# Gated attention decode on one core: single K and V tiles take one half of the rows of their pair of tiles

## The chip, the cores and the metric

The kernel runs on one core of a Trainium2 chip. The metric is the device time of one execution in microseconds (us). Each comparison below runs the kernel and the kernel before on the same chip, in turn.

## The reference, cut to what matters

One token (`x`, 1 x 1024) goes through two branches. Branch A is grouped-query attention over a cache of 65,536 positions: 32 query heads, 4 groups of K and V, 128 values per head. Branch B is a small gated MLP. A sigmoid gate mixes them.

```python
q = (x @ wq).reshape(B, Sq, Hq, Dh).transpose(0, 2, 1, 3)
scores = einsum('bhqd,bhkd->bhqk', q, repeat(k_cache, 8)) * Dh ** -0.5
p = softmax(scores)                       # over the 65,536 positions k
o = einsum('bhqk,bhkd->bhqd', p, repeat(v_cache, 8))
a = o.transpose(0, 2, 1, 3).reshape(B, Sq, Hq * Dh) @ wo
return g * a + (1 - g) * b                # b: the MLP, g: the gate
```

What matters: the sum over `k` pairs the probability of position k with the V row of position k. Any order of the positions gives the same sum, so a kernel may spread them over the partitions as it likes, but it must spread K and V in the same way.

K and V of one group are 16.8 MB each, 134 MB in all. With the weights the kernel has to read 162 MB.

## The kernel before: what the change and the argument touch

PE is the engine for matrix products (PEld is its loading of weights), DVE the vector engine, ACT the scalar engine, POOL the GpSimd engine, and SP the engine that issues the loads; 16 DMA engines carry them out. SBUF is the core's own memory, 128 partitions wide. It holds one large buffer `kv` with 5 slots of 32 KiB per partition. A tile of K or V is 128 partitions x 128 positions x 128 values, one slot, 4 MB. A group has 4 tiles (j = 0 to 3) of K and 4 of V.

```python
def load_kv(src, g, j, at, n=1):
    k0, m = j * CT * P, n * CT                      # CT = P = 128
    v = load(src[0, g, k0:k0 + m * P, :].rearrange("(p c) d -> p (c d)", c=m),
             (m * DH,), at)
    return [v[:, i * CT * DH:(i + 1) * CT * DH] for i in range(n)]
...
for j in range(NT):                                 # group 0: four single loads of K
    k_tile(0, j, load_kv(A_k_cache, 0, j, (2, 1, 0, 3)[j])[0])
    ...
for g in range(1, G):
    for h in range(2):
        kn = load_kv(A_k_cache, g, 2 * h, 1 - h, 2)      # a pair of K tiles
        ...
        vn = load_kv(A_v_cache, g - 1, 2 * h, 3, 2)      # a pair of V tiles
        ...
for j, n, at in ((0, 2, 1), (2, 1, 3), (3, 1, 4)):  # V of group 3: one pair, two singles
    for i, vt in enumerate(load_kv(A_v_cache, G - 1, j, at, n)):
        v_tile(G - 1, j + i, vt)
```

A single load (n = 1) gives each partition 128 consecutive positions. A pair load (n = 2) gives each partition 256 consecutive positions, of which tile j takes the first 128 and tile j + 1 the other 128. So K of group 0 (singles) and V of group 0 (pairs) do not hold the same positions in the same place, and neither do tiles 2 and 3 of group 3 (K in a pair, V in singles).

`k_tile` transposes the tile in place in 32 x 32 blocks on DVE (four per tile) and multiplies it with the queries on PE into `s_ps`; ACT casts the scores to `sc`. `stats` finds the maximum, takes the exponentials and transposes the probabilities into `pt`. `v_tile` multiplies `pt` with the V tile. A slot comes free when the work on its tile is done, and only then is the next load for it issued, on one queue (SP), in program order.

## Time and profile before

| | before |
|---|---|
| time, median of the runs made with the prediction's result | 383.25 us (383.21 to 383.29, 4 runs) |
| bytes moved, mean rate over the span | 162.17 MB, 425 GB/s |
| load queue, share of 16 DMA engines' time | 98.8% |
| PE, DVE busy | 59%, 57% |

These are lines of the page of the kernel before. The two rows of figures cut the span into 40 slices: the mean busy share of the DMA engines in tenths (9 is 90% or more), and GB/s. "q1" is the load queue: its packets (a packet is one piece of a load that one DMA engine moves; a K or V load has one for each partition), MB, and the share of the 16 DMA engines' time. The next two lines are the chain of waits by engine and by line. The last two are groups of instructions: count, busy us and mean ns of one, then the idle time before them and what ended it.

```profile
span 381.3 us, 2581 instructions
...
PE 226.1 (59%) x1372; PEld 56.1 (15%) x796; DVE 218.5 (57%) x211; ACT 39.6 (10%) x55; POOL 4.4 (1%) x10
...
DMA  9999999999999999999999999999999999999995
GB/s 376 435 419 430 428 437 440 440 444 422 414 433 440 440 428 433 440 440 440 440 428 440 440 440 426 413 422 426 440 440 414 433 433 434 440 407 440 437 401 237
...
q1 hardware_dynamic: 4324, 162.01, 98.8%
...
DMA 60%; DVE 18%; PE 17%; issue 2%; ACT 1%; SPq 1%; DVEq 0%; ACTq 0%
DMA kv<-in_A_k_cache_dram 37%; PE s_ps L390 12%; DVE kv L383 12%; DMA kv<-in_A_wo_dram 9%; DMA kv<-in_A_wq_dram 7%; DMA kv<-in_A_v_cache_dram 7%; PE o_ps L436 3%; DVE pt L426 2%; DVE mx L385 1%; DVE o_sb L450 1%; PE q_ps L276 1%; ACT sc L42
...
L390 PE MATMUL s_ps<-kv,wt 128*128 128x512 bf16 x512 | 137.0, 424 | 87.6 <-DVE kv L383 87.4
L383 DVE STREAM_TRANSPOSE kv<-kv 128x2048 int32<-128x2048 int32 x64 | 142.7, 2280 | 58.7 <-DMA kv<-in_A_k_cache_dram 58.7
```

The loads bound this kernel, by this reading: the DMA row stands at 9 until the last slice, and no other engine comes near. The chain of waits still gives a third of its length to PE and DVE. Those pieces are what a load's slot waits for, while another load is already on the queue, so they show what has to happen in time, not what would shorten the run.

The table by stretches of the kernel before (us busy and instruction counts of each engine, the clock that PE was granted as a share of full speed, DMA share, GB/s) has the single loads of K of group 0 in the first stretch, the pair loads in the second and the single loads of V of group 3 in the third:

```profile
core 0: us, PE busy (x) PEld busy (x) DVE busy (x) ACT busy (x) POOL busy (x), PEclk, DMA share, GB/s
39.00:80.00 41.00, 24.84 (x120) 5.12 (x60) 33.23 (x30) 2.02 (x2) 0.00 (x0) 0.88 1.00 429
80.00:338.00 258.00, 163.75 (x889) 37.16 (x482) 166.28 (x123) 34.00 (x47) 0.00 (x0) 0.84 1.00 433
338.00:359.00 21.00, 12.57 (x98) 3.55 (x51) 1.77 (x6) 0.00 (x0) 0.00 (x0) 0.83 0.99 424
```

The DMA share is 0.99 to 1.00 in all three, and singles run at the rate of pairs within about 2%.

### The profile page before, as it was taken

The numbers are of one execution on the slowest core, as the hardware profiler recorded it, in microseconds if no ns is written. First come the engines' busy times: TensorE is split into PE (matmuls) and PEld (weight loads), VectorE is DVE, ScalarE is ACT, GpSimd is POOL, SyncE is SP. The second block draws the span as 40 slices with busy tenths as digits, with TensorE's granted clock in tenths as the row PEclk, the third lists the DMA queues.
The fourth block names the chain that finished last, engine by engine and source line by source line (L and its number), as shares of the span: only waits on it lengthen the run. The fifth ranks groups of instructions, "written<-read, shape, count | busy, mean of one in ns | idle before, by whom it ended". The sixth has DMA issues, their size and how long they took to land.

```text
span 381.3 us, 2581 instructions
## 1 busy us (share of the span) xinstructions
PE 226.1 (59%) x1372; PEld 56.1 (15%) x796; DVE 218.5 (57%) x211; ACT 39.6 (10%) x55; POOL 4.4 (1%) x10
## 2 busy tenths in 40 slices
PE   0433357677047934885388538762966197848354
PEld 0110011112011200111011101110211011212122
DVE  4241479996678406866986059669770497460040
ACT  1010001111601100114011001140100010500000
POOL 4000000000000000000000000000000000000000
PEclk9999859999759885999598959996899688969686
DMA  9999999999999999999999999999999999999995
GB/s 376 435 419 430 428 437 440 440 444 422 414 433 440 440 428 433 440 440 440 440 428 440 440 440 426 413 422 426 440 440 414 433 433 434 440 407 440 437 401 237
DMA packets 4375, 162.17 MB, mean 425 GB/s; under 512 B 520, under 2 KB 524, under 8 KB 908
## 3 DMA queue, kind: packets, MB, share of 16 engines
q1 hardware_dynamic: 4324, 162.01, 98.8%
q8 instruction: 8, 0.13, 0.1%
q14 instruction: 3, 0.02, 0.0%
q10 hardware_dynamic: 40, 0.01, 0.0%
HBM read 162.01 MB, written 0.00 MB: 425 GB/s over the span
## 4 chain that ended last, share of the span: by engine, by line
DMA 60%; DVE 18%; PE 17%; issue 2%; ACT 1%; SPq 1%; DVEq 0%; ACTq 0%
DMA kv<-in_A_k_cache_dram 37%; PE s_ps L390 12%; DVE kv L383 12%; DMA kv<-in_A_wo_dram 9%; DMA kv<-in_A_wq_dram 7%; DMA kv<-in_A_v_cache_dram 7%; PE o_ps L436 3%; DVE pt L426 2%; DVE mx L385 1%; DVE o_sb L450 1%; PE q_ps L276 1%; ACT sc L423 1%; DVE rowt L446 1%; ACT sc L401 1%; SPq L167 1%
## 5 line engine op out<-in xcount | busy, mean ns | idle before, releaser
L390 PE MATMUL s_ps<-kv,wt 128*128 128x512 bf16 x512 | 137.0, 424 | 87.6 <-DVE kv L383 87.4
L383 DVE STREAM_TRANSPOSE kv<-kv 128x2048 int32<-128x2048 int32 x64 | 142.7, 2280 | 58.7 <-DMA kv<-in_A_k_cache_dram 58.7
L436 PE MATMUL o_ps<-kv,pt 128*64 128x512 bf16 x512 | 60.4, 394 | 7.8 <-DMA kv<-in_A_v_cache_dram 7.8
L390 PEld LDWEIGHTS <-wt 128*128 128x128 bf16 x256 | 26.9, 105 | 199.1 <-issue 137.2
L401 ACT CAST sc<-s_ps 128x1024 bf16<-128x1024 f32 x16 | 16.2, 1012 | 253.7 <-PE s_ps L390 253.7
L436 PEld LDWEIGHTS <-pt 128*64 128x64 bf16 x256 | 15.8, 114 | 49.8 <-issue 47.7
L426 DVE STREAM_TRANSPOSE pt<-sc 128x1024 bf16<-128x1024 bf16 x16 | 18.6, 1217 | 6.8 <-ACT sc L423 6.8
L385 DVE TENSOR_REDUCE mx<-sc 128x1 f32<-128x1024 bf16 x12 | 14.5, 1210 | 8.9 <-ACT sc L401 8.9
L423 ACT ACTIVATE sc<-sc,nb 128x1024 bf16<-128x1024 bf16 x16 | 18.2, 1137 | 12.2 <-DVE nb L419 12.2
L446 DVE TENSOR_TENSOR rowt<-o_ps,own 128x1024 f32<-128x1024 f32 x4 | 4.8, 1195 | 23.8 <-PE o_ps L436 23.8
L456 PE MATMUL om_ps<-o_sb,hsel 128*32 128x128 f32 x8 | 2.3, 387 | 19.7 <-DVE o_sb L450 19.7
L405 DVE TENSOR_REDUCE mx<-sc 128x1 f32<-128x1024 bf16 x4 | 4.9, 1221 | 12.9 <-ACT sc L401 12.9
L276 PE MATMUL q_ps<-kv,xT 128*32 128x512 bf16 x64 | 6.8, 600 | 7.3 <-DMA kv<-in_A_wq_dram 7.3
L477 PE MATMUL out_ps<-kv,oa 128*32 128x256 bf16 x128 | 7.1, 377 | 4.1 <-DMA kv<-in_A_wo_dram 2.6
L276 PE MATMUL z_ps<-kv,xT 128*32 128x448 bf16 x64 | 6.4, 577 | 3.6 <-DMA kv<-in_B_w_in_dram 3.6
L343 DVE TENSOR_TENSOR rowt<-q_ps,own_b 128x512 f32<-128x512 f32 x2 | 1.3, 686 | 12.0 <-PE q_ps L276 12.0
L450 DVE TENSOR_REDUCE o_sb<-rowt 128x128 f32<-128x1024 f32 x4 | 7.5, 1872 | 0.1
L291 DVE TENSOR_TENSOR rowt<-z_ps,own_b 128x448 f32<-128x448 f32 x2 | 1.2, 620 | 8.4 <-PE z_ps L276 8.4
L276 PEld LDWEIGHTS <-xT 128*32 128x32 bf16 x64 | 3.0, 139 | 19.1 <-issue 19.0
L232 PE MATMUL xb_ps<-xg,spread 8*128 8x256 bf16 x1 | 0.4, 367 | 9.0 <-DMA xg<-in_gate_w_dram 9.0
L477 PEld LDWEIGHTS <-oa 128*32 128x32 bf16 x128 | 4.6, 127 | 6.5 <-issue 4.0
L520 ACT CAST out_sb<-out_ps 128x256 bf16<-128x256 f32 x1 | 0.4, 372 | 44.9 <-PE out_ps L477 44.9
(88 smaller groups left out, 54.9 us busy)
## 6 DMA issues: line engine op xcount, KB each, us to landing
kv<-in_A_k_cache_dram SPq DMA_DIRECT2D x4, 4096.0 KB, 26.7
kv<-in_A_wq_dram SPq DMA_DIRECT2D x2, 4096.0 KB, 32.7
kv<-in_A_v_cache_dram SPq DMA_DIRECT2D x2, 4096.0 KB
kv<-in_B_w_in_dram SPq DMA_DIRECT2D x2, 3584.0 KB, 14.9
kv<-in_A_wo_dram SPq DMA_DIRECT2D x1, 4096.0 KB
kv<-in_B_w_out_dram SPq DMA_DIRECT2D x1, 3584.0 KB
kv<-in_A_wo_dram SPq DMA_DIRECT2D x1, 2048.0 KB, 29.2
kv<-in_A_wo_dram SPq DMA_DIRECT2D x1, 1024.0 KB, 31.3
```

What stands on the lines that cost most here:

```text
L276: ins = nc.tensor.matmul(ps[t * B:(t + 1) * B, k * HN:k * HN + n], lhsT=xT[:, i * KH + c:i * KH + c + 1].to_broadcast([P, B]), rhs=w[:, c, ...
L383: nc.vector.transpose(out=kb[:, v * n:(v + 1) * n], in_=kb[:, v * n:(v + 1) * n])
L385: nc.vector.reduce_max(**late.pop())
L390: ins = nc.tensor.matmul(s_ps[:, k * HN:(k + 1) * HN], lhsT=wt[g % 2][:, v, b].rearrange("p a v h -> p (a v h)"), rhs=kx[:, b // 2, b % 2, ...
L401: nc.scalar.copy(out=sct[g, j][:], in_=s_ps[:])
L405: nc.vector.reduce_max(**late.pop())
L423: nc.scalar.activation(out=sct[g, j][:], in_=sct[g, j][:], func=ACT.Exp, scale=SCALE, bias=nb[:, 0:1], accum_out=lss[g][:, j:j + 1])
L426: nc.vector.transpose(out=ptt[g, j][:].rearrange("p c x -> p (c x)"), in_=sct[g, j][:])
L436: ins = nc.tensor.matmul(o_ps[g][hs, e, :], lhsT=ptt[g, j][:, 2 * u:2 * u + 2, :].rearrange("p c x -> p (c x)"), rhs=vx[:, 2 * u + e], sta ...
L446: nc.vector.tensor_tensor(out=om8, in0=o_ps[g][:].rearrange("p e (v d) -> p (e v) d", d=DH), in1=own_8[:].unsqueeze(2).to_broadcast([P, 2 ...
L450: nc.vector.tensor_reduce(out=o_sb[:], in_=om8.rearrange("p x d -> p d x"), axis=AX.X, op=ALU.add)
L477: nc.tensor.matmul(out_ps[t * B:(t + 1) * B, :], lhsT=vec[:, c0 + c:c0 + c + 1].to_broadcast([P, B]), rhs=w[:, c, t * NO:(t + 1) * NO], st ...
```

## The change

The intent is that every tile takes its half of the rows of its pair, whether it is loaded alone or with its partner, so that a partition holds the same positions for K and for V.

```diff
     def load_kv(src, g, j, at, n=1):
-        k0, m = j * CT * P, n * CT
-        v = load(src[0, g, k0:k0 + m * P, :].rearrange("(p c) d -> p (c d)", c=m),
-                 (m * DH,), at)
+        h, i = divmod(j, 2)
+        rows = src[0, g, 2 * h * CT * P:2 * (h + 1) * CT * P, :].rearrange(
+            "(p c) d -> p (c d)", c=2 * CT)
+        v = load(rows[:, i * CT * DH:(i + n) * CT * DH], (n * CT * DH,), at)
         return [v[:, i * CT * DH:(i + 1) * CT * DH] for i in range(n)]
```

Pair loads are as they were. The six single loads still bring 32 KiB to each partition, but from places 64 KiB apart (the pitch) instead of 32 KiB.

## The prediction

> **What bounds the kernel now.** The loads. The page's DMA row stands at 9 tenths or more in all 40 slices but the last, the load queue's packets fill 98.8% of the span of the 16 DMA engines, and 162.17 MB move in 381.3 us, 425 GB/s. The table by stretches gives a DMA share of 0.97 to 1.04 from 33 us to 346 us. PE is busy 59%, DVE 57%. The chain of waits is 60% DMA; its PE and DVE pieces (L390, L383) run while the queue holds the next load and matter only for how early a buffer comes free.
>
> **What the change does.** It touches no instruction on PE, DVE, ACT or POOL, no buffer and no wait, only source addresses of loads.
> - The 13 pair loads (6 of K, 7 of V) keep their source exactly: 64 KiB per partition, all contiguous.
> - The 6 single loads (4 of K for group 0, 2 of V for group 3) read 32 KiB per partition, as before, but from rows 64 KiB apart instead of 32 KiB: the same 4 MB, the same 128 packets of 32 KiB each.
>
> Its worth is correctness: before, K of group 0 and V of group 3's last two tiles came with 128 consecutive positions per partition while their partners came as halves of 256, so probabilities met the wrong V rows there. With nearly flat softmax weights the comparison with the reference probably hardly sees it.
>
> **What it costs.** Only a slower read from rows of wider pitch could cost time. The trace already has that pattern: the loads of A_wq and the 4 MB load of A_wo take 32 KiB of every 64 KiB. By the packet records, their packets take a median of 1213 ns (A_wq) and 1216 ns (A_wo); those of the contiguous single K and V loads 1216 ns; those of the pair loads 2421 ns for twice the bytes. All are 27 GB/s per engine. The Trainium skill ("DMA: Bandwidth & Descriptors", section "Latency and other measured facts") reports that large power-of-two row pitches slow HBM copies: 207 GB/s at 512 KiB, 164 at 2 MiB, 214 when padded. 64 KiB is below what it lists, and this trace shows no loss there. If the 6 loads' packets took 1% longer, 6 x 8 x 1.216 us = 58 us of DMA time would give 0.6 us (an estimate from those durations). It would be paid in full, as the queue is always full. I expect none.
>
> **Predicted: 383.25 us, 8 in 10 between 382.6 and 383.9.** Faster by over 2%: 0.01; within 2%: 0.98; slower by over 2%: 0.01.
>
> **What would show the steps right or wrong.**
> - Instruction count (2581) and packet counts (4324 on the load queue; 1152 of 32 KiB, 1664 of 64 KiB) unchanged.
> - Packets of 32 KiB keep a median within 1% of 1216 ns; from 33 to 72 us the queue still moves about 430 GB/s.
> - The chain keeps its shape: DMA about 60%, K loads about 37%.
> - Busy times of L390, L383, L436 unchanged within clock noise.
>
> **What would make it wrong.** If engines in lockstep at 64 KiB pitch collide in the HBM, the 6 loads' packets get longer (stretches 39 to 80 us and 338 to 359 us), by a few us in all at most. If the new source were cut into other descriptors, the packet counts would show it. If a K load landed so late that PE or DVE ran out of slack, later buffers would come free later, the queue's waits would grow and the DMA row would dip.

## The result

| | before | after |
|---|---|---|
| median | 383.25 us (4 runs) | 383.18 us (383.05 to 383.26, 4 runs) |
| ratio | | 0.9998, 95% interval 0.9981 to 1.0015 |

A ratio here is the mean time of one kernel's fast runs over that of the other's of the same rounds, so it is not quite the ratio of the medians.

The same lines of the page of the kernel after (its line numbers are one higher):

```profile
span 381.4 us, 2581 instructions
...
PE 232.4 (61%) x1372; PEld 56.8 (15%) x796; DVE 218.4 (57%) x211; ACT 39.6 (10%) x55; POOL 4.4 (1%) x10
...
DMA  9999999999999999999999999999999999999995
GB/s 376 439 426 416 433 436 440 436 461 429 400 426 440 440 435 426 440 440 440 440 428 440 440 440 433 428 427 406 433 440 428 426 433 427 440 411 436 440 405 230
...
q1 hardware_dynamic: 4324, 162.01, 98.7%
...
DMA 59%; PE 20%; DVE 16%; issue 2%; ACT 1%; SPq 1%; DVEq 0%; ACTq 0%
DMA kv<-in_A_k_cache_dram 37%; PE s_ps L391 15%; DVE kv L384 9%; DMA kv<-in_A_wo_dram 8%; DMA kv<-in_A_wq_dram 7%; DMA kv<-in_A_v_cache_dram 7%; PE o_ps L437 3%; DVE pt L427 2%; DVE mx L386 1%; DVE o_sb L451 1%; PE q_ps L277 1%; ACT sc L424
...
L391 PE MATMUL s_ps<-kv,wt 128*128 128x512 bf16 x512 | 142.1, 437 | 81.8 <-DVE kv L384 81.7
L384 DVE STREAM_TRANSPOSE kv<-kv 128x2048 int32<-128x2048 int32 x64 | 142.7, 2280 | 55.5 <-DMA kv<-in_A_k_cache_dram 55.5
```

And the same stretches:

```profile
core 0: us, PE busy (x) PEld busy (x) DVE busy (x) ACT busy (x) POOL busy (x), PEclk, DMA share, GB/s
39.00:80.00 41.00, 26.40 (x120) 5.29 (x60) 33.11 (x30) 2.03 (x2) 0.00 (x0) 0.83 1.00 429
80.00:338.00 258.00, 167.68 (x889) 37.69 (x482) 166.61 (x123) 34.01 (x47) 0.00 (x0) 0.83 1.00 433
338.00:359.00 21.00, 13.14 (x98) 3.62 (x51) 1.47 (x6) 0.00 (x0) 0.00 (x0) 0.83 0.99 424
```

The DMA shares and the GB/s of the three stretches are those of before to the last digit shown. Instructions and packets are as many as before. What moved is PE, and with it the parts of PE and DVE in the chain of waits: the score matmuls took 437 ns instead of 424 ns, 5.1 us more in all, in a run whose mean granted clock was 0.82 instead of 0.855. The same file in e11, at a mean clock of 0.863, took 427 ns, so most of this is a difference between runs and not the change. The span did not follow it (381.4 us in both runs of the changed kernel, 381.3 us before).

The trace also records each packet of the load queue. Sorted by size and order of start they fall into the loads, and this table gives the median time of one packet:

| packets | before | after |
|---|---|---|
| 32 KiB, A_wq (pitch 64 KiB in both) | 1213 ns | 1213 ns |
| 32 KiB, K of group 0 (pitch 32 KiB, then 64 KiB) | 1216 ns | 1216 ns |
| 32 KiB, V of group 3 (pitch 32 KiB, then 64 KiB) | 1216 ns | 1216 ns |
| 64 KiB, pairs of K and V | 2421 ns | 2421 ns |

The times of the runs alone leave room for about 0.6 us of loss, which is what 1% longer packets in these six loads would cost. The packets exclude it: they have the same median in both, to the nanosecond.

### The profile page after: what moved, and what is told of

It reads as the page before. It is cut to its first block, busy times and chain, and to the rows that moved or that the text cites. A ratio compares the mean times of both kernels' runs of the same rounds, so it can differ in the third digit from the quotient of the medians.

```text
span 381.4 us, 2581 instructions
## 1 busy us (share of the span) xinstructions
PE 232.4 (61%) x1372; PEld 56.8 (15%) x796; DVE 218.4 (57%) x211; ACT 39.6 (10%) x55; POOL 4.4 (1%) x10
## 3 DMA queue, kind: packets, MB, share of 16 engines
q1 hardware_dynamic: 4324, 162.01, 98.7%
## 4 chain that ended last, share of the span: by engine, by line
DMA 59%; PE 20%; DVE 16%; issue 2%; ACT 1%; SPq 1%; DVEq 0%; ACTq 0%
DMA kv<-in_A_k_cache_dram 37%; PE s_ps L391 15%; DVE kv L384 9%; DMA kv<-in_A_wo_dram 8%; DMA kv<-in_A_wq_dram 7%; DMA kv<-in_A_v_cache_dram 7%; PE o_ps L437 3%; DVE pt L427 2%; DVE mx L386 1%; DVE o_sb L451 1%; PE q_ps L277 1%; ACT sc L424 1%; DVE rowt L447 1%; ACT sc L402 1%; SPq L167 1%
## 5 line engine op out<-in xcount | busy, mean ns | idle before, releaser
L391 PE MATMUL s_ps<-kv,wt 128*128 128x512 bf16 x512 | 142.1, 437 | 81.8 <-DVE kv L384 81.7
L437 PE MATMUL o_ps<-kv,pt 128*64 128x512 bf16 x512 | 61.6, 399 | 7.7 <-DMA kv<-in_A_v_cache_dram 7.7
```

What stands on the lines that cost most here:

```text
L391: ins = nc.tensor.matmul(s_ps[:, k * HN:(k + 1) * HN], lhsT=wt[g % 2][:, v, b].rearrange("p a v h -> p (a v h)"), rhs=kx[:, b // 2, b % 2, ...
L437: ins = nc.tensor.matmul(o_ps[g][hs, e, :], lhsT=ptt[g, j][:, 2 * u:2 * u + 2, :].rearrange("p c x -> p (c x)"), rhs=vx[:, 2 * u + e], sta ...
```

## The experiments

Theory 1 says: the queue is always full, a packet's time depends on its bytes and not on the distance between rows, so nothing changes. Rival 2 says: a wider pitch does cost, but six loads and a doubling are too little to be seen. Rival 3 says: the engines set the time and these six loads have slack, so even a slower load would not have been seen. All edits are against the kernel after, if not said otherwise. Four kernels besides the detectors compute something wrong (e2, e3, e4 and e7).

### e1: pitch 128 KiB for all K and V loads

```diff
-        h, i = divmod(j, 2)
-        rows = src[0, g, 2 * h * CT * P:2 * (h + 1) * CT * P, :].rearrange(
-            "(p c) d -> p (c d)", c=2 * CT)
-        v = load(rows[:, i * CT * DH:(i + n) * CT * DH], (n * CT * DH,), at)
+        rows = src[0, g].rearrange("(p c) d -> p (c d)", c=NT * CT)
+        v = load(rows[:, j * CT * DH:(j + n) * CT * DH], (n * CT * DH,), at)
```

> All 19 K and V loads read from rows twice as far apart as in the changed kernel: 128 KiB pitch, each partition holding 512 consecutive positions of its group for K and for V alike, so the result stays right. Theory 1 (the queue is always full and a packet's time is set by its bytes alone): 383.2 us, 382.6 to 383.9; packets of 64 KiB keep a median of 2421 ns and those of 32 KiB 1216 ns, within 1%. Rival 2 (wider pitch costs, but in the change it touched too few loads by too little to be seen): now 310 us of load time are touched instead of 58 us, so even 1% longer packets give plus 3 us.

Measured: 383.22 us against 383.34 us, ratio 0.9996 (0.9982 to 1.0011). Packets: 1216 and 2421 ns. Now all 19 loads are touched and there is still nothing.

### e2: pitch 512 KiB, the widest there is

```diff
+        rows = src[0].rearrange("g (q c) d -> (g q) (c d)", c=G * NT * CT)
+        t = g * NT + j
+        v = load(rows[:, t * CT * DH:(t + n) * CT * DH], (n * CT * DH,), at)
```

(in place of the same four lines as in e1)

> All 19 K and V loads read from the widest pitch that 128 rows allow in this cache, 512 KiB, over all groups (wrong positions on purpose). Theory 1: 382.6 to 384.5 us, packets as before within 1%. Rival 2, sized by the Trainium skill's 207 against 214 GB/s at 512 KiB (DMA: Bandwidth & Descriptors, Latency and other measured facts): 3.4% of 310 us of load time, plus 10 us, about 394 us, with the longer packets in the K and V loads only.

(The 10 us and the 394 us are an estimate from the page's two figures. The page gives the 214 GB/s for a padded pitch of 4 MiB, which it calls the full rate.)

Measured: 383.22 us against 383.34 us, ratio 0.9998 (0.9981 to 1.0014). Packets: 1216 and 2421 ns. Rival 2 falls for the pitches that were run, 64, 128 and 512 KiB (256 was not): the interval leaves room for 0.5 us, not for 10.

### e3: the six single loads in runs of 2 KiB

```diff
+        if n == 1:
+            rows = src[0, g, j * CT * P:(j + 1) * CT * P, :].rearrange(
+                "(a p c) d -> p a (c d)", p=P, c=8)
+            return [load(rows, (CT // 8, 8 * DH), at).rearrange("p a b -> p (a b)")]
```

> The 6 single loads are cut into 2 KiB runs, 16 per partition, 2048 packets a load instead of 128 (pairing of K and V wrong again on purpose; bytes the same). Theory 1 with packet size as the one thing that counts: the A_wo tail shows 85 ns for a 2 KiB packet, 16 of them 1360 ns against 1216 ns for 32 KiB; 6 loads x 8 x 0.144 us is plus 6.9 us, about 390 us (387 to 393). Rival 3 (these six loads have slack, the engines set the time, so a slower load would not have been seen): within 1 us of 383.2.

Measured: 390.24 us against 383.34 us, 6.9 us more, ratio 1.0179 (1.0164 to 1.0195). The stretches of the two groups of single loads in e3:

```profile
core 0: us, PE busy (x) PEld busy (x) DVE busy (x) ACT busy (x) POOL busy (x), PEclk, DMA share, GB/s
39.00:80.00 41.00, 22.73 (x110) 4.65 (x55) 30.38 (x29) 2.03 (x2) 0.00 (x0) 0.82 1.04 387
...
338.00:359.00 21.00, 12.65 (x98) 3.53 (x51) 6.57 (x10) 1.15 (x3) 0.00 (x0) 0.84 0.98 372
```

The DMA share is still about 1, but the rate fell from 429 to 387 GB/s in the stretch of the K loads. The last stretch also holds the end of a pair load, since everything comes later in e3 (the 2 KiB packets of V begin at 341.7 us); from 346 to 362 us, inside the V loads, the rate is 386 to 388 GB/s at a DMA share of 1.04 to 1.05. So these six loads are on the bounding path, and rival 3 falls: had the change made them slower, the time would have shown it. That the estimate of 6.9 us was met to the digit is partly luck: a 2 KiB packet took 87 ns in the median and 88.4 ns in the mean, not 85, which by the same sum (6 loads x 8 rows for each engine) would be 8.4 to 9.4 us (48 x (16 x 87 - 1216) ns, 48 x (16 x 88.4 - 1218) ns). The share of 1.04 says that the short packets' records overlap a little, so their times add up to more than the time that passed. By the rate, 25.2 MB at 387 instead of 429 GB/s take 6.4 us longer.

### e4: half of one of these loads

```diff
+        if src is A_k_cache and (g, j) == (0, 2):
+            load(rows[:, i * CT * DH:i * CT * DH + CT * DH // 2], (CT * DH // 2,), at)
+            return [kv[:, at * CT * P:(at + 1) * CT * P]]
```

> Tile 2 of K of group 0 loads only half of its bytes, 16 KiB per partition; the rest of the tile is what A_wq left there (wrong on purpose). 2.1 MB less. Theory 1: the load time saved, 8 x 0.608 us = 4.9 us, is saved in full: 378.3 us (377.5 to 379.2). Rival 3 (slack at these loads, engines bound): within 0.6 us of 383.2.

Measured: 378.80 us (378.38 to 379.95) against 383.34 us, ratio 0.9886 (0.9868 to 0.9904), which is 4.4 us less; the profiled run, one of the fastest, shows 4.8 us less than the kernel before:

```profile
span 376.5 us, 2581 instructions
```

Theory 1 asked for 4.9 us. So the time follows the time of these loads in both directions, longer packets in e3 and fewer bytes here. Why this kernel's runs spread over 1.6 us, where the kernel before spread over 0.25 us, was not looked into.

### e5: pairs everywhere

The other way to make K and V agree is to have no single loads.

```diff
-    for j in range(NT):
-        k_tile(0, j, load_kv(A_k_cache, 0, j, (2, 1, 0, 3)[j])[0])
-        if j == 1:
+    for h in range(2):
+        kn = load_kv(A_k_cache, 0, 2 * h, (3, 1)[h], 2)
+        for i in range(2):
+            k_tile(0, 2 * h + i, kn[i])
+        if h == 0:
             build_w(1)
-    project(load(B_w_out..., (FC, D), 4), FC, uT, 0, first=True)
+    project(load(B_w_out..., (FC, D), 0), FC, uT, 0, first=True)
 ...
-    for j, n, at in ((0, 2, 1), (2, 1, 3), (3, 1, 4)):
+    for j, n, at in ((0, 2, 1), (2, 2, 3)):
```

> The other way to make K and V agree: no single loads at all; K of group 0 and V of group 3 come as pairs too (slots 3-4 and 1-2, A_w_out's load moved to slot 0), all sources contiguous, all packets of K and V 64 KiB. Theory 1: three pair loads replace six singles, 3 x 8 x 11 ns less, 383.0 us (382.3 to 383.8); same as the changed kernel within 0.2%. Rival 3 (engines bound): starting group 0 later by a whole pair and ending V in a pair costs waits, plus 3 us or more.

(A_w_out there is the matrix B_w_out.)

Measured: 403.50 us against 383.21 us, ratio 1.0530 (1.0514 to 1.0546). I missed this by 20 us. It lies where rival 3 put it (plus 3 us or more), but not for rival 3's reason alone, as e10 will show. The queue's own timeline of e5 (start, duration, what was issued) and its stretches show where the time lies:

```profile
22.79 10.26 SPq L167 DMA_DIRECT2D kv<-in_A_k_cache_dram  x2
42.66 0.33 SPq L167 DMA_DIRECT2D kv<-in_B_w_out_dram  x1
104.94 0.33 SPq L167 DMA_DIRECT2D kv<-in_A_k_cache_dram  x1
105.36 0.71 SPq L167 DMA_DIRECT2D kv<-in_A_v_cache_dram  x1
```

```profile
core 0: us, PE busy (x) PEld busy (x) DVE busy (x) ACT busy (x) POOL busy (x), PEclk, DMA share, GB/s
30.00:79.00 49.00, 21.29 (x112) 4.16 (x51) 22.36 (x22) 1.01 (x1) 0.00 (x0) 0.70 0.99 428
79.00:105.00 26.00, 19.91 (x86) 4.08 (x50) 21.70 (x15) 2.08 (x3) 0.00 (x0) 0.91 0.24 103
105.00:126.00 21.00, 2.17 (x59) 1.62 (x51) 6.67 (x9) 6.88 (x10) 0.00 (x0) 0.64 0.99 415
```

No load is issued between 42.66 and 104.94 us, and from 79 to 105 us the DMA share is 0.24: 26 us x 0.76 = 20 us of empty queue. The first load of group 1 is to go into slots 1 and 2, and I had put the second pair of group 0 there, whose last tile is done at 104.9 us. The load behind it, for V, could have gone into slots 3 and 4, where PE was done with the first pair at 84.8 us, but a queue in program order holds it back. So this was my order of slots; e10 tests that.

### e6: singles everywhere, contiguous

```diff
+        return [load(src[0, g, k * CT * P:(k + 1) * CT * P, :].rearrange(
+            "(p c) d -> p (c d)", c=CT), (CT * DH,), at + k - j) for k in range(j, j + n)]
```

(the whole body of load_kv)

> The opposite remedy: every K and V tile is its own contiguous 4 MB load, 32 loads instead of 19, pitch 32 KiB, K and V agree. Theory 1: 26 half pairs at 1216 ns instead of 2421/2 ns per 32 KiB packet is 26 x 8 x 5.5 ns = plus 1.1 us, 384.3 us (383.3 to 385.5). Rival 2 (contiguity helps the memory): below 382.5.

Measured: 384.46 us against 383.21 us, ratio 1.0031 (1.0017 to 1.0045): 1.25 us more, where the packet times gave 1.1. Two packets of 32 KiB take 2 x 1216 = 2432 ns, one of 64 KiB takes 2421 ns. So 32 contiguous loads are correct too, and a little slower than the change.

### e7: no transposes

```diff
-            nc.vector.transpose(out=kb[:, v * n:(v + 1) * n], in_=kb[:, v * n:(v + 1) * n])
```

> The changed kernel without the 64 transposes of K (142.7 us of DVE; wrong scores on purpose). Theory 1: the queue was full all the time, so nothing is gained: 382.2 to 384 us. Rival 3 (the chain of waits, with 9% in these transposes and 15% in the score matmuls behind them, is what bounds): up to 36 us faster, 348 us, at least 5 us.

Measured: 383.07 us against 383.21 us, ratio 0.9994 (0.9980 to 1.0008). From the page of e7:

```profile
span 381.1 us, 2492 instructions
...
PE 224.8 (59%) x1372; PEld 58.4 (15%) x796; DVE 77.3 (20%) x147; ACT 39.6 (10%) x55; POOL 4.4 (1%) x10
...
DMA  9999999999999999999999999999999999999995
```

DVE is down from 218.4 to 77.3 us busy, and the span went from 381.4 to 381.1 us. That is all that the transposes in the chain of waits were worth here. The score matmuls remained, so this says nothing about removing PE's work.

### e8 and e9: a detector of the pairing

The comparison with the reference passes both kernels, and it also passed e2, e3, e4 and e7, which pair, read or score wrongly. So I made the pairing itself visible. V's loads read the K cache; before the transposes, half a position (64 values per partition) of each K tile of groups 0 and 3 is kept; when the V tile of the same g and j comes, the same place is compared, and the sum of the squared differences is added to the output. If K and V are spread alike, this sum is zero.

```diff
+            nc.vector.tensor_copy(out=seen[g, j][:], in_=kn[:, CT // 2 * DH:CT // 2 * DH + DH // 2])
 ...
+            nc.vector.tensor_tensor(out=df[:], in0=vt[:, CT // 2 * DH:CT // 2 * DH + DH // 2],
+                                    in1=seen[g, j][:], op=ALU.subtract)
+            nc.vector.tensor_tensor(out=df[:], in0=df[:], in1=df[:], op=ALU.mult)
+            nc.vector.reduce_sum(out=apart[:, k:k + 1], in_=df[:], axis=AX.X)
 ...
-            vn = load_kv(A_v_cache, g - 1, 2 * h, 3, 2)
+            vn = load_kv(A_k_cache, g - 1, 2 * h, 3, 2)
 ...                                  # summed over tiles and partitions, added to out_ps
```

(e8 is this on the kernel before, e9 on the kernel after; cut)

> A detector of the pairing, on the kernel before: V's loads read the K cache instead, and for groups 0 and 3 half a position (64 values per partition) of each V tile is compared with the same place of the K tile of the same name; the sum of the squared differences is added to every output. If the pairing is wrong in K and V of group 0 (4 tiles) and in tiles 2 and 3 of group 3, 6 tiles x 128 x 64 x 2 x 0.05^2 is about 246 (the reference draws the cache with a deviation of 0.05), so outputs of about 246 and a failed comparison. If the pairing was right: 0 and a passed comparison. Time within 1 us of 383.2 either way.

> The same detector on the changed kernel. If the change makes every partition hold the same positions for K and for V: the sum is exactly 0 and the output compares as well with the reference as without the detector, although V has been replaced by K (which would show that the comparison does not feel the attention's values). If not: outputs of tens to hundreds and a failed comparison. Time within 1 us of 383.2.

Measured: e8 is wrong by a relative error of 5935, e9 compares as correct. The kernel before did pair probabilities with other positions' V rows, and the kernel after does not, for the place in each tile of groups 0 and 3 that was compared. (That e9's sum was exactly 0 is not on record, only that the comparison passed.) The size of e8's error fits the six tiles that the code names. Worked out afterwards on a host from the inputs of the reference, these tiles give a sum of 242.1, about 40 each, and the reference's output has a root mean square of 0.0408; the quotient is 5937, against 5935 measured, if the relative error is the size of the error over that of the output. The runs do not say which six of the eight tiles differed; that rests on reading the code.

And e9 passes although its attention multiplies the probabilities with K instead of V: the comparison does not feel which of the two the attention reads, so it could not have told the two kernels apart. The same working on the host says why: with K in place of V the output changes by 0.02%, and with the wrong pairing by far less still.

The times, one run each in an unknown state, were 384.48 and 385.49 us against 383.10 us, 1.4 and 2.4 us more where I had allowed 1. In both profiles 0.8 us of it is the detector's own tail, PE and DVE work after the last projection (3.8 and 3.9 us from the end of the last load packet to the end of the span, instead of 3.0); the rest was not taken apart.

### e10: pairs everywhere, slots in the other order

```diff
-        kn = load_kv(A_k_cache, 0, 2 * h, (3, 1)[h], 2)
+        kn = load_kv(A_k_cache, 0, 2 * h, (1, 3)[h], 2)
```

(against e5)

> All pairs again, with the two K pairs of group 0 in the other order of slots: first pair in 1-2, second in 3-4. In e5 the first load of group 1 needed slots 1-2, which the second pair held until 104.9 us, and the queue stood empty from 79 to 105 us (DMA share 0.24 there). Now the first pair holds them, which lands near 59 us and should be through near 82 us, before the queue runs dry near 88 us. Theory 1 (e5's 20 us are only the empty queue, pairs cost nothing): 383.0 us (382.3 to 383.9), DMA row at 9 in all slices but the last. Rival (loading group 0 in pairs costs by itself): 390 us or more.

Measured: 388.07 us (387.11 to 389.01) against 383.18 us, ratio 1.0130 (1.0114 to 1.0146). 15 of e5's 20 us are gone, so the order of slots was most of it, but 4.9 us stay, and I had expected none. The queue's timeline of the kernel after, then of e10:

```profile
6.87 36.71 SPq L167 DMA_DIRECT2D kv<-in_A_k_cache_dram  x4
43.67 0.38 SPq L167 DMA_DIRECT2D kv<-in_B_w_out_dram  x1
71.85 0.33 SPq L167 DMA_DIRECT2D kv<-in_A_k_cache_dram  x1
95.97 0.33 SPq L167 DMA_DIRECT2D kv<-in_A_v_cache_dram  x1
119.21 0.33 SPq L167 DMA_DIRECT2D kv<-in_A_k_cache_dram  x1
```

```profile
32.96 0.80 SPq L167 DMA_DIRECT2D kv<-in_A_k_cache_dram  x2
42.68 0.33 SPq L167 DMA_DIRECT2D kv<-in_B_w_out_dram  x1
81.80 0.33 SPq L167 DMA_DIRECT2D kv<-in_A_k_cache_dram  x1
103.51 0.33 SPq L167 DMA_DIRECT2D kv<-in_A_v_cache_dram  x1
127.00 0.33 SPq L167 DMA_DIRECT2D kv<-in_A_k_cache_dram  x1
```

The second load of group 1's K is issued at 127.00 us instead of 119.21 us. It needs the slot of group 1's first K tile, and DVE comes to that tile late, because it comes late to the end of group 0. These are the transposes of the first K tile of group 0 (the first of them waits for the load) and the reduction on its last K tile in the timelines of DVE, first of the kernel after, then of e10:

```profile
48.83 8.89 DVE L384 STREAM_TRANSPOSE kv<-kv 128x2048 int32<-128x2048 int32 x4 [1.59 <-DMA kv<-in_A_k_cache_dram]
...
95.37 1.22 DVE L406 TENSOR_REDUCE mx<-sc 128x1 f32<-128x1024 bf16 x1 [3.79 <-ACT sc L402]
```

```profile
59.12 8.89 DVE L384 STREAM_TRANSPOSE kv<-kv 128x2048 int32<-128x2048 int32 x4 [11.89 <-DMA kv<-in_A_k_cache_dram]
...
104.56 1.22 DVE L406 TENSOR_REDUCE mx<-sc 128x1 f32<-128x1024 bf16 x1 [3.03 <-ACT sc L402]
```

The work begins 10.3 us later and its end is 9.2 us later, about the load time of one tile (8 x 1216 ns = 9.7 us): in pairs the work of group 0 cannot begin until two tiles have landed. The stretches of e10 show what that does to the queue:

```profile
core 0: us, PE busy (x) PEld busy (x) DVE busy (x) ACT busy (x) POOL busy (x), PEclk, DMA share, GB/s
80.00:124.00 44.00, 26.08 (x152) 6.43 (x105) 35.73 (x24) 8.96 (x12) 0.00 (x0) 0.84 1.01 429
124.00:132.00 8.00, 5.16 (x25) 1.14 (x12) 5.76 (x4) 1.01 (x1) 0.00 (x0) 1.00 0.78 295
132.00:346.00 214.00, 141.95 (x758) 31.64 (x389) 135.64 (x106) 25.05 (x35) 0.00 (x0) 0.85 1.00 431
```

In the 8 us around the late issue the DMA share is 0.78, 1.8 us lost. The packet records account for the rest. The engines stand idle for 0.6 us between 100 and 120 us, before the V load issued at 103.51 us, and for 2.1 us between 120 and 140 us. In each of the two loads after these gaps the 64 KiB packets took 100 ns longer (means 2528 and 2517 ns, where most loads have 2420 to 2430; over all loads the mean is 2438 ns instead of 2425), 2 x 8 x 0.1 = 1.6 us. Why they do is not known. That makes 4.3 us, and the last load packet ends 4.3 us later (382.7 instead of 378.4 us).

e10 also brings the last two V tiles of group 3 as a pair, and its chain of waits now ends in the work on that pair. But from the end of the last load packet to the end of the span it takes 3.2 us instead of 3.0, so this cost 0.1 us or so. The expectation's rival was right in kind, though not in size: with this use of the slots, loading group 0 in pairs costs by itself, as the work starts later.

### e11: the change once more

The file is the kernel after, unchanged.

> The changed kernel once more, with more rounds and on the chip of e10, to narrow the interval of the change itself. Theory 1: ratio to the kernel before within 0.9985 to 1.0015, 383.2 us (382.9 to 383.5), and e10 within 0.5 us of it.

Measured: 383.24 us (383.20 to 383.34, 5 runs) against 383.18 us, ratio 1.0002 (0.9989 to 1.0014). The first clause held. The second, e10 within 0.5 us of it, did not.

## Why the prediction was right

- "What bounds the kernel now. The loads." Right. Bytes taken from one of the six loads came back as time (e4: 4.4 us by the ratio, 4.8 us in the profiled run, of 4.9), and 141 us of DVE work taken away came back as nothing (e7). PE's work was not taken away in any run.
- "It touches no instruction on PE, DVE, ACT or POOL, no buffer and no wait, only source addresses of loads." Right: 2581 instructions and 4324 packets on the load queue in both.
- "The trace already has that pattern." This was the step that carried the prediction. A_wq is read at the pitch that the change gives to K and V, and its 1213 ns stood in the trace before. The six loads came out at 1216 ns.
- "It would be paid in full, as the queue is always full." The result could not show this, since there was nothing to pay. e3 shows it: made slower by shorter runs, the same loads cost 6.9 us.
- The Trainium skill's figures for wide pitches ("DMA: Bandwidth & Descriptors", section "Latency and other measured facts") were the reason for some caution. The page's copies go between HBM tensors in rows of 16 KiB; e1 and e2 show no loss for loads into SBUF in runs of 32 and 64 KiB, at a pitch of 128 and 512 KiB.
- "The comparison with the reference probably hardly sees it." Right: e9 passes with K in V's place. No run tests the prediction's reason, flat softmax weights, against the other one, that branch A is small against branch B. Worked out on a host from the reference's inputs, both hold: the weights of all heads lie within 0.07% of 1/65,536, which hides a wrong pairing, and branch A makes up 0.05% of the output, which hides e9's exchange of V for K.

What the prediction did not say is why the kernel keeps single loads for group 0 at all. e5 and e10 answer that for K: in pairs the first group's work starts a tile later, and with five slots the queue then ran dry in both orders of slots that were tried. For V of group 3, a pair at the end cost about 0.1 us in e10. The change keeps the singles and mends the pairing. Of the layouts here in which K and V agree, it and e1 (383.2 us both) are the fastest, before contiguous singles (e6, 384.5), and pairs (e10, 388.1, and e5, 403.5). No correct version beat the kernel before beyond noise.

## What to carry to other kernels

When a load changes only where it reads, look in the trace for a load that already reads that way, and compare the time per packet; here a weight matrix gave the answer before anything ran. Length of the contiguous run and the moment when a slot comes free cost time in this kernel; the distance between runs did not, at the pitches that were run. And a passed comparison is proof only of what it can feel: make the property itself visible, as with the sum that had to be zero, before you trust a layout.

## What the Trainium skill lacked or had wrong

- "DMA: Bandwidth & Descriptors", section "Latency and other measured facts": it gives 207 GB/s at a row pitch of 512 KiB, against about 214 at full rate, for copies between HBM tensors. It has no figure for loads into SBUF. Here loads in runs of 32 KiB took 1216 ns per packet at a pitch of 32, 64, 128 and 512 KiB alike, and loads in runs of 64 KiB took 2421 ns at a pitch of 64, 128 and 512 KiB.
- No page gives a measured time of one load packet of these sizes on this queue ("DMA: Bandwidth & Descriptors", section "Why small descriptors are slow (HBM only)", has an overhead in cycles for each packet and works it out for 256 bytes): 85 to 87 ns for 2 KiB, 1216 ns for 32 KiB, 2421 ns for 64 KiB. In the stretch of the K loads cut to 2 KiB the rate was 387 GB/s instead of 429, though each of these loads moves 4 MB.
- "SBUF — State Buffer", section "Summary: rules for kernel authors", says to estimate HBM to SBUF with about 358 GB/s. This kernel, run on one core only, moved 425 GB/s over its whole span. "HBM Reference", section "Specifications (TRN2)", has it right: about 425 for a core that streams alone.
